# Expert 0's rows numbered by themselves; the routing of all experts computed at once inside expert 0's second block

## The chip, the core and the metric

The kernel runs on one core of one Trainium2 chip. The metric is the device time of one execution in microseconds (us), taken as the median over several timed executions. Besides the timed ones there is one profiled execution, whose trace is the source of every row quoted below. A core has five engines that run in parallel, each through its own instruction queue in order: TensorE (PE; PEld is its weight load), VectorE (DVE), ScalarE (ACT), GpSimd (POOL) and SyncE (SP, which here only starts DMAs). They wait for each other through semaphores.

## The reference, cut to what matters

Three stages follow one another: a packed attention, a mixture of experts with two of eight experts for each row, and a dense gated block.

```python
def _moe_ref(x, w_gate, w_noise, noise, w1, w2):      # x: 2304 rows of 512, the attention's output
    noisy_logits = x @ w_gate + np.log1p(np.exp(x @ w_noise)) * noise     # 2304 x 8
    top2 = np.argpartition(-noisy_logits, 2, axis=1)[:, :2]
    top2_l = np.take_along_axis(noisy_logits, top2, axis=1)
    top2_w = np.exp(top2_l - top2_l.max(-1, keepdims=True)); top2_w /= top2_w.sum(-1, keepdims=True) + 1e-09
    for e in range(8):
        for k in range(2):
            mask = top2[:, k] == e
            h = np.maximum(x[mask] @ w1[e], 0.0)
            out[mask] += top2_w[mask, k, None] * (h @ w2[e])
def _moe2_ref(x, w_in, w_out):
    h = x @ w_in
    return (h * (1 / (1 + np.exp(-h)))) @ w_out
```

## The kernel before

The 2304 rows are 18 row tiles of 128. Attention makes the row tiles two at a time (`unpacked`): scores `s`, a softmax on DVE, ACT and POOL (tiles `mx`, `sd`), transposes `a2p`, and the product `xp`, which gives a row tile (`xr`, written to the DRAM tensor `xs`) and its 16 gate and noise columns (`lg`). Attention's products are plain float32, the experts' are split into a high and a low part (three matmuls in float32r).

Routing (`route`) turns `lg` into a numbering. For each row: noisy logits `ny`, the two largest (`V.max`, `V.max_index`), one-hot rows `oh` and `ob`; a matmul with a triangle of ones (`rk`) counts the earlier rows of the same expert, so each row has a place in its expert's list. The list is turned inside out by matmuls `ip` of two one-hot factors (`oa`, 128 wide, and `oc`, 40 wide): place p of expert e then holds the row's index (`idx`). Routing runs in two chunks, row tiles 0 to 10 (`EARLY = 11`) and 11 to 17. From the same numbers come `slots` and `gates`, used only when the experts' results are combined, some 400 us later.

An expert's list has 640 places, handled as block A (2 tiles, 256 rows) and block B (3 tiles, 384 rows). A block gathers its rows from `xs` by an indirect DMA that POOL issues (`fetch`, one DMA for each tile of 128), transposes them on TensorE (`tps`), splits them into high and low (`xh` on ACT, `xl` on DVE; `xha` is block A's, `xhb` block B's), and then runs 8 steps f: `first` (12 matmuls into `hps`), `relu_split` (`hh` on ACT, `hl` on DVE), `second` (3 matmuls for each tile into `acc`; `wa4` to `wa7` are their weights, two steps to each). Block A of expert 0 needs only rows of the first chunk; block B needs the numbering of all rows.

Before the change, chunk one's numbering covers all experts, in steps spread over the last attention slots; chunk two's is spread over the steps of expert 0's block A; the rows of block B and of expert 1's block A are fetched after step 4 of block A. The scheduler of the framework then orders each engine's instructions. Expert 0's blocks use the weights `wa`, expert 1's `wb`; during expert 0's block B the weights of expert 1 are loaded and split (`split`, 1024 wide, ACT and DVE).

## Time and profile before

| | us |
|---|---|
| timed executions, median of 3 (lowest, highest) | 1002.8 (1000.08, 1003.62) |
| profiled execution, its own time | 994.48 |
| its span, first to last instruction | 992.6 |
| TensorE busy in the span | 962.6 |

The span is 1.9 us shorter than the profiled execution's own time, and that execution is 8.3 us shorter than the timed median, so terms are worked out on the trace and added to the median. A row of the timeline gives start, duration, engine, line, operation, what it writes and reads, its count, and in brackets how long its engine was idle before it and what ended the wait.

### The profile page before, as it was taken

The numbers are of one execution on the slowest core, as the hardware profiler recorded it, in microseconds if no ns is written. First come the engines' busy times: TensorE is split into PE (matmuls) and PEld (weight loads), VectorE is DVE, ScalarE is ACT, GpSimd is POOL, SyncE is SP. The second block draws the span as 40 slices with busy tenths as digits, with TensorE's granted clock in tenths as the row PEclk, the third lists the DMA queues.
The fourth block names the chain that finished last, engine by engine and source line by source line (L and its number), as shares of the span: only waits on it lengthen the run. The fifth ranks groups of instructions, "written<-read, shape, count | busy, mean of one in ns | idle before, by whom it ended". The sixth has DMA issues, their size and how long they took to land.

```text
span 992.6 us, 14383 instructions
## 1 busy us (share of the span) xinstructions
PE 962.6 (97%) x5584; PEld 825.5 (83%) x5584; DVE 447.7 (45%) x871; ACT 346.4 (35%) x631; POOL 312.8 (32%) x345
## 2 busy tenths in 40 slices
PE   6989799999999999999999999999999999999996
PEld 4767589999999999999999988888888888888885
DVE  3536763666767676676734448312212221111111
ACT  3657323443434433343423344322222222222221
POOL 2155214252424353352200127333323322222221
PEclk9979699999999999999999999999999999999999
DMA  8995223575657666665623455101011010001001
GB/s 234 249 265 165 92 86 106 183 239 179 217 187 231 191 216 215 199 222 184 193 94 118 141 174 163 54 22 43 22 51 35 23 53 1 1 1 43 0 1 46
DMA packets 82298, 122.49 MB, mean 123 GB/s; under 512 B 16432, under 2 KB 49200, under 8 KB 82224
## 3 DMA queue, kind: packets, MB, share of 16 engines
q1 hardware_dynamic: 74416, 101.05, 32.2%
q0 software_dynamic: 7520, 19.93, 6.9%
q8 instruction: 46, 0.75, 0.3%
q10 hardware_dynamic: 288, 0.52, 0.2%
q14 instruction: 28, 0.23, 0.1%
HBM read 93.17 MB, written 28.31 MB: 122 GB/s over the span
## 4 chain that ended last, share of the span: by engine, by line
PE 90%; DVE 4%; DMA 3%; ACT 1%; SPq 1%; issue 1%; DVEq 0%; ACTq 0%
PE hps L208 14%; PE hps L210 14%; PE hps L209 14%; PE acc L220 14%; PE acc L219 14%; PE acc L221 14%; PE xp L461 1%; PE s L430 1%; PE tps L157 1%; DMA vm<-in_v_dram 1%; PE s L363 1%; DMA km<-in_k_dram 1%; PE kp L352 1%; DVE rt_oa L535 1%; DMA raw<-wf_out 0%
## 5 line engine op out<-in xcount | busy, mean ns | idle before, releaser
L176 POOL DMA_INDIRECT xg<-xs,idx x120 | 126.6, 1055 | 195.5 <-DVE xturn L185 148.0
L751 POOL TENSOR_TENSOR gl<-sg,gh 128x512 fp32r<-128x512 f32 (+1 forms) x80 | 95.3, 1193 | 253.8 <-ACT gh L750 238.2
L232 ACT ACTIVATE hh<-hps 128x384 fp32r<-128x384 f32 (+1 forms) x128 | 56.1, 438 | 260.0 <-PE hps L210 256.3
L747 DVE TENSOR_TENSOR sg<-hps,sg 128x512 f32<-128x512 f32 (+1 forms) x80 | 50.7, 634 | 196.3 <-ACT sg L746 196.1
L233 DVE SCALAR_TENSOR_TENSOR hl<-hps,hh 128x384 fp32r<-128x384 f32 (+1 forms) x128 | 62.5, 488 | 122.9 <-ACT hh L232 122.3
L746 ACT ACTIVATE sg<-hps 128x512 f32<-128x512 f32 (+1 forms) x80 | 44.2, 553 | 190.2 <-PE hps L210 189.9
L750 ACT ACTIVATE gh<-sg 128x512 fp32r<-128x512 f32 (+1 forms) x80 | 47.1, 589 | 78.4 <-DVE sg L747 78.3
L737 POOL DMA_INDIRECT y<-ys,slots x36 | 36.5, 1014 | 110.7 <-DVE hl L233 72.5
L740 DVE TENSOR_SCALAR y<-y,gates 128x512 f32<-128x512 f32 x18 | 10.8, 602 | 38.2 <-DMA y<-ys,slots 38.2
L461 PE MATMUL xp<-ppBD,a2T 128*128 128x272 f32 (+1 forms) x80 | 25.5, 462 | 1.6 <-ACT xr L51 0.8
L741 DVE SCALAR_TENSOR_TENSOR y<-y,gates,y 128x512 f32<-128x512 f32 x18 | 15.7, 871 | 24.0 <-DMA y<-ys,slots 24.0
L690 DVE SCALAR_TENSOR_TENSOR t<-raw,t 128x512 int32<-128x512 int32 x32 | 22.2, 693 | 0.9
L196 POOL DMA_INDIRECT xg<-xs,idx x10 | 9.7, 969 | 40.9 <-DVE idx_f L556 19.4
L691 DVE SCALAR_TENSOR_TENSOR t<-raw,t 128x512 int32<-128x512 int32 x32 | 22.1, 691 | 0.9
L185 DVE STREAM_TRANSPOSE xturn<-xg 128x512 f32<-128x512 f32 x30 | 21.2, 707 | 2.6 <-DMA wf_in<-t 1.5
L687 ACT ACTIVATE t<-raw 128x512 f32<-128x512 f32 x32 | 21.2, 662 | 0.1
L430 PE MATMUL s<-ppT,qT 128*128 128x64 f32 x128 | 19.6, 309 | 0.0
L430 PEld LDWEIGHTS s<-ppT,qT 128*128 128x128 f32 x128 | 19.0, 227 | 0.6
L208 PE MATMUL hps<-xha,wa3h 128*128 128x256 f32 (+1 forms) x56 | 17.7, 316 | 1.8 <-DVE sg L747 1.8
L160 DVE TENSOR_TENSOR xla<-tps,xha 128x512 fp32r<-128x512 f32 x14 | 9.6, 690 | 21.1 <-ACT xha L159 21.0
L53 DVE COPY ysb<-acc 128x512 f32<-128x512 f32 x24 | 16.4, 683 | 4.8 <-PE acc L221 4.8
L352 PE MATMUL kp<-ident,km 128*128 128x128 f32 x64 | 12.0, 327 | 6.2 <-DMA km<-in_k_dram 5.8
(450 smaller groups left out, 2987.2 us busy)
## 6 DMA issues: line engine op xcount, KB each, us to landing
raw<-in_moe_w_dram SPq DMA_DIRECT2D x56, 512.0 KB, 3.9
ys<-ysb SPq DMA_DIRECT2D x40, 256.0 KB, 3.6
raw<-in_moe_w_in_dram SPq DMA_DIRECT2D x16, 512.0 KB, 4.2
raw<-in_moe_w_out_dram SPq DMA_DIRECT2D x16, 512.0 KB, 4.2
xs<-xr SPq DMA_DIRECT2D x18, 256.0 KB, 2.1
km<-in_k_dram SPq DMA_DIRECT2D x8, 512.0 KB, 7.5
vm<-in_v_dram SPq DMA_DIRECT2D x8, 512.0 KB, 7.5
qm<-in_q_dram SPq DMA_DIRECT2D x8, 512.0 KB, 7.1
```

Of the source, the lines that this page charges most:

```text
L176: G.indirect_dma_start(out=xg[:, g * P:(g + 1) * P], out_offset=None, in_=xs[:, :].rearrange("n (a f) -> (n a) f", a=4), in_offset=bass.In ...
L208: T.matmul(ps, wh[:, c, s], xh[:, c, :n], start=c == 0, stop=False)
L209: T.matmul(ps, wh[:, c, s], xl[:, c, :n], start=False, stop=False)
L210: T.matmul(ps, wl[:, c, s], xh[:, c, :n], start=False, stop=c == 3)
L219: T.matmul(y, hh[:, s], wh[:, f % 2, :], start=f == 0, stop=False)
L220: T.matmul(y, hh[:, s], wl[:, f % 2, :], start=False, stop=False)
L221: T.matmul(y, hl[:, s], wh[:, f % 2, :], start=False, stop=f == last)
L232: A.activation(hh, ps, AF.Relu)
L233: V.scalar_tensor_tensor(hl, ps, 0.0, hh.bitcast(F32), op0=OP.max, op1=OP.subtract)
L430: T.matmul(s2[:, :, h, :], qT[:, h, :], ppT[b, h // 4][:, h % 4], start=True, stop=True)
L747: V.tensor_tensor(sg, ps, sg, op=OP.mult)
L751: G.tensor_tensor(gl, sg, gh.bitcast(F32), op=OP.subtract)
```

## The change

- Chunk steps now number expert 0 alone (`first_rows`): a row counts if its expert 0 logit reaches its second largest, so `max_index`, `oh` and the 8-wide counts fall away; `rk` is n wide, `oc` 5 wide, `oa` one per row tile. Noisy logits stay in `ny`.
- Chunk one runs in one go in attention slot 9, and block A's rows are fetched at slot 12; chunk two's steps run after the last slot and give rows for block B alone (`idx0[:, TA:ET]`, 3 tiles), fetched before block A's loop in program order.
- A new `route()` inside expert 0's block B does what the old routing did for all 18 row tiles at once, with one `oa` and one `oc` instruction for each row tile and choice (36 of each, in tile `pc`). Expert 1's block A rows are fetched at step 4 of block B, those of its block B at step 6.
- `slots` and `gates` move there too; some constants are kept in working tiles.

```diff
-            for i in range(n):
-                V.max_index(i8[:, i, :], m8[:, i, :], ny[:, i, :])
-            ch = chosen[:, t0:t0 + n, :]
...
-            T.matmul(rk, ones, sbase[:, None, :].to_broadcast([P, n, E]), start=True, stop=False)
-            T.matmul(rk, ones, seen_b[:, None, :].to_broadcast([P, n, E]), start=False, stop=False)
-            T.matmul(rk, before, ob, start=False, stop=n == 1)
...
+            m0 = tl([], "m0", BF)
+            V.tensor_tensor(m0, yn[:, :, 0], m8[:, :, 1], op=OP.is_ge)
+            yield
+            rk = pMx.tile([P, n], F32, name="rk", tag="m")
+            T.matmul(rk, before, m0, start=True, stop=False)
...
+            V.scalar_tensor_tensor(sf, rk, -63.5, m0, op0=OP.add, op1=OP.mult)
...
+            for j in range(n):
+                V.tensor_scalar(oa[:, j, :], iota_lo, lo[:, j:j + 1], None, op0=OP.is_equal)
+            ip = pMx.tile([P, ET], F32, name="ip", tag="m")
+            for j in range(n):
+                T.matmul(ip, oa[:, j, :], oc[:, j, :], start=j == 0, stop=j == n - 1)
+            yield
+            if t0 == 0:
+                V.tensor_scalar(idx0[:, 0:TA], ip[:, 0:TA], float(-MID), float(MID), op0=OP.max, op1=OP.add)
...
+            else:
+                V.tensor_tensor(row0, row0, ip, op=OP.add)
+                V.tensor_scalar(idx0[:, TA:ET], row0[:, TA:ET], 0.0, float(N - 1), op0=OP.max, op1=OP.min)
...
-            if slot >= START2[5] + LAG2[3]:
-                run(r0, RSTEP)
+            if slot == START2[5] + LAG2[3]:
+                for _ in r0:
+                    pass
+            if slot == START2[-1]:
...
+                for j, xg in enumerate(fetch(xs[0:EARLY * P, :], idx0, 0, TA)):
+                    transposed(plain(xg), *X["a"], j)
+        for _ in r1:
             pass
...
+        for j, xg in enumerate(fetch(xs[:, :], idx0, TA, TB)):
+            transposed(plain(xg), *X["b"], j)
         for f in expert_block(0, 0, TA, X["a"]):
-            run(r1, 2)
...
+            pass
...
+                for i in range(NT):
+                    V.max(m8[:, i, :], ny[:, i, :])
+                for i in range(NT):
+                    V.max_index(i8[:, i, :], m8[:, i, :], ny[:, i, :])
...
+                            V.tensor_scalar(pc[:, j, c, 0:P], iota_lo, lo[:, t, c:c + 1], None, op0=OP.is_equal)
+                            V.tensor_scalar(pc[:, j, c, P:P + E * ET], iota_hi, hi[:, t, c:c + 1], rowv[:, t:t + 1],
+                                            op0=OP.is_equal, op1=OP.mult)
...
+                if e == 0:
+                    for _ in range(1 if f else 3):
+                        next(routing, None)
+                    if f == 4:
+                        box["a"] = fetch(xs[:, :], idx, ET, TA)
+                    if f == 6:
+                        for j, xg in enumerate(box["a"]):
+                            transposed(plain(xg), *X["a"], j)
...
-                if f == 5:
+                if f == (5 if e else 6):
```

**TensorE's queue from chunk one's counts to expert 0's block A.** Before (`rk` counts, `ip` inverts, `tps` and `hps` are block A's):

```order
L513 MATMUL rk<-rt_ob_1372,before 128x88
...
L461 MATMUL xp<-ppBD_185,a2T_1462 128x272
...
L430 MATMUL s_1634<-ppT_195,qT 128x2x32 x4
...
L452 MATMUL a2p<-ident,sd_1586 128x128 x4
...
L542 MATMUL ip<-rt_oc_1452,rt_oa_1451 128x40
...
L461 MATMUL xp<-ppBD_193,a2T_1675 128x272
...
L157 MATMUL tps<-ident,xg 128x128 x8
...
L208 MATMUL hps<-xha,wa0h 128x256
```

Now the same stretch:

```order
L502 MATMUL rk<-rt_m_1357,before 128x11
...
L506 MATMUL rk<-rt_m_1357,ones 128x1
L522 LDWEIGHTS rt_oa_1382
L522 MATMUL ip<-rt_oc_1379,rt_oa_1382 128x5
...
L388 MATMUL pp<-vm,a1T 32x64 x16
...
L460 MATMUL xp<-ppBD_184,a2T_1471 128x272
...
L156 MATMUL tps<-ident,xg 128x128 x8
...
L207 MATMUL hps<-xha,wa0h 128x256
```

Between `rk` and `ip` stood attention's `xp`, `s` and `a2p`; now nothing does, and the attention work follows `ip`. Eight `xp` products and six `a2p` transposes of the last row tiles now stand behind block A's first `hps`.

**GpSimd's queue around the fetch of block A's rows** (`ppBD<-px` are copies of attention's first half, `sd` a step of its softmax, `xg` the fetched rows). Before:

```order
L119 TENSOR_TENSOR wa7l<-raw,wa7h 128x256 x4
L397 COPY ppBD_197<-px 32x64 x4
L447 TENSOR_TENSOR sd_1586<-sd_1586,mx_1584 128x512
L196 DMA xg<-xs,idx_102 128x512 x2
L447 TENSOR_TENSOR sd_1645<-sd_1645,mx_1643 128x512
```

Now:

```order
L118 TENSOR_TENSOR wa7l<-raw,wa7h 128x256 x4
L396 COPY ppBD_196<-px 32x64 x4
L195 DMA xg<-xs,idx_99 128x512 x2
L446 TENSOR_TENSOR sd_1561<-sd_1561,mx_1559 128x512
L446 TENSOR_TENSOR sd_1625<-sd_1625,mx_1623 128x512
```

The two fetches moved ahead of one softmax step and stand right behind the four copies. The `px` that these copy needs the `pp` which now stands behind `ip` on TensorE.

**TensorE's queue from block A's last step to block B.** Before (`xhb` is block B's operand, `wa7` belongs to the last step):

```order
L221 MATMUL acc<-wa7h,hl 128x512 x2
L157 MATMUL tps<-ident,xg 128x128 x4
L219 MATMUL acc<-wa7h,hh 128x512
...
L221 MATMUL acc<-wa7h,hl 128x512 x2
L208 MATMUL hps<-xhb,wa0h 128x384
```

Now:

```order
L522 MATMUL ip<-rt_oc_1779,rt_oa_1782 128x5
L218 MATMUL acc<-wa7h,hh 128x512
...
L220 MATMUL acc<-wa7h,hl 128x512 x2
L752 LDWEIGHTS ones
L752 MATMUL rk<-sbase,ones 128x144
L156 MATMUL tps<-ident,xg 128x128 x12
L207 MATMUL hps<-xhb,wa0h 128x384
```

The transposes of block B's three tiles stood among block A's steps, with the last `tps` there being expert 1's; now they stand behind all of block A, six `acc` matmuls after the `ip` whose result gives their row indices.

## Rows read from the trace of the kernel before

**Rows 1.** The page: busy time by engine, and the chain that ended last.

```profile
PE 962.6 (97%) x5584; PEld 825.5 (83%) x5584; DVE 447.7 (45%) x871; ACT 346.4 (35%) x631; POOL 312.8 (32%) x345
PE 90%; DVE 4%; DMA 3%; ACT 1%; SPq 1%; issue 1%; DVEq 0%; ACTq 0%
```

**Rows 2.** Windows: length, busy PE, PEld, DVE, ACT, POOL (count), granted clock, DMA share, GB/s.

```profile
93.90:97.00 3.10, 3.10 (x71) 2.72 (x67) 2.99 (x7) 1.53 (x6) 3.06 (x6) 1.00 0.18 63
93.90:124.00 30.10, 23.76 (x198) 17.62 (x194) 24.31 (x102) 10.79 (x29) 12.38 (x21) 0.72 0.29 95
124.00:153.50 29.50, 28.79 (x230) 23.74 (x228) 17.98 (x85) 7.89 (x21) 4.76 (x5) 1.00 0.23 72
153.50:190.00 36.50, 36.50 (x194) 33.34 (x195) 13.76 (x19) 11.65 (x19) 11.43 (x11) 1.00 0.47 136
101.50:118.60 17.10, 13.05 (x80) 9.70 (x79) 14.66 (x45) 4.08 (x9) 4.31 (x6) 0.50 0.25 79
```

**Rows 3.** Windows of 1 us around changes of the granted clock.

```profile
53.00:54.00 1.00, 0.00 (x0) 0.00 (x0) 0.00 (x0) 0.80 (x1) 0.00 (x0) 0.88 1.00 255
64.00:65.00 1.00, 1.00 (x28) 0.83 (x30) 0.00 (x0) 0.91 (x3) 1.00 (x3) 1.00 1.09 359
101.00:102.00 1.00, 0.65 (x12) 0.51 (x10) 1.00 (x6) 0.34 (x1) 0.71 (x3) 0.77 0.00 0
118.00:119.00 1.00, 0.63 (x3) 0.21 (x3) 0.97 (x3) 0.00 (x0) 0.74 (x1) 0.70 0.64 139
```

**Rows 4.** Timeline of VectorE, chunk one's numbering.

```profile
92.95 0.20 DVE L483 TENSOR_SCALAR rt_h<-rt_w 128x88 f32<-128x88 f32 x1
...
97.53 0.84 DVE L498 MAX8 rt_m<-rt_ny 128x8 f32<-128x8 f32 x11
...
99.85 0.76 DVE L578 TENSOR_TENSOR rt_ex<-rt_m 128x11 f32<-128x11 f32 x1
...
109.97 3.29 DVE L535 TENSOR_TENSOR rt_oa<-iota_lo,rt_lo 128x768 f16<-128x768 f16 x4
```

**Rows 5.** Timeline of TensorE, end of attention to block B.

```profile
91.14 1.08 PE L461 MATMUL xp<-ppBD,a2T 128*128 128x272 f32 x4
...
101.52 0.56 PE L515 MATMUL rk<-rt_ob,ones 128*128 128x80 bf16 x10
...
120.70 1.04 PE L157 MATMUL tps<-ident,xg 128*128 128x128 f32 x8
...
137.95 0.55 PE L542 MATMUL ip<-rt_oc,rt_oa 128*128 128x40 f16 x8 [0.55 <-DVE rt_oa L535]
...
140.70 0.49 PE L560 MATMUL i<-idx_f,ident 128*32 128x40 f32 x32
...
153.46 0.44 PE L208 MATMUL hps<-xhb,wa0h 128*128 128x384 f32 x1
...
157.73 0.39 PE L219 MATMUL acc<-wa4h,hh 128*128 128x512 f32 x1
157.96 0.40 PE L220 MATMUL acc<-wa4l,hh 128*128 128x512 f32 x1
```

**Rows 6.** Timeline of GpSimd, copies and fetches.

```profile
100.52 1.27 POOL L397 COPY ppBD<-px 32x64 f32<-32x64 f32 x4
...
139.24 0.98 POOL L196 DMA_INDIRECT xg<-xs,idx  x1 [19.43 <-DVE idx_f L556]
140.52 0.95 POOL L196 DMA_INDIRECT xg<-xs,idx  x1 [0.31 <-issue]
```

**Rows 7.** The fetch's line, L196: DMA to landing.

```profile
DMA to landing us min/median/max: 3.4/3.5/4.0
```

**Rows 8.** Timeline of ScalarE and VectorE: the split of fetched rows.

```profile
121.74 1.08 ACT L159 ACTIVATE xha<-tps 128x512 fp32r<-128x512 f32 x2
...
123.06 0.68 DVE L160 TENSOR_TENSOR xla<-tps,xha 128x512 fp32r<-128x512 f32 x1
```

**Rows 9.** Groups of VectorE instructions from 98.2 to 99.84 us: busy, mean ns.

```profile
L500 DVE FIND_INDEX8 rt_i<-rt_m,rt_ny 128x8 uint32<-128x8 f32 x11 | 1.5, 160 | 0.0
```

More of the change, by code (lines that the diff above doesn't have):

```diff
@@ L89, in body @@
     slots = const.tile([P, NT, 2], I32)
-    seen = const.tile([P, E], F32)
-    V.memset(seen, 0.0)
-    seen_b = const.tile([P, E], BF)
-    V.memset(seen_b, 0.0)
+    ny = const.tile([P, NT, E], F32)
     idx_f = const.tile([P, E * ET], F32)
@@ L96, in body @@
     idx = const.tile([P, E * ET], I32)
-    idx0 = const.tile([P, TA], I32)
+    idx0 = const.tile([P, TA + TB], I32)
     idx4 = const.tile([P, 4, E * ET], I32)
@@ L101, in body @@
         V.memset(quad[32 * a:32 * a + 32], float(a))
-    few = const.tile([P, E], F32)
+    few = const.tile([P, 1], F32)
+    cnt = const.tile([P, E], F32)
+    most = const.tile([P, 1], I32)
     M = {"pin": False, "w": 384, "hb": 3}
@@ L513, in route @@
-            T.matmul(rk, before, ob, start=False, stop=n == 1)
+            rk = pMx.tile([P, n], F32, name="rk", tag="m")
+            T.matmul(rk, before, m0, start=True, stop=False)
+            if t0:
+                T.matmul(rk, ones, seen_b.to_broadcast([P, n]), start=False, stop=False)
             for j in range(n - 1):
-                T.matmul(rk[:, j + 1:, :], ones, ob[:, j:j + 1, :].to_broadcast([P, n - 1 - j, E]),
-                         start=False, stop=j == n - 2)
-            rs = tl([E], "rs")
@@ L518, in route @@
-            V.tensor_scalar(rs, rk, -63.5, None, op0=OP.add)
-            V.tensor_tensor(oh, oh, rs[:, :, None, :].to_broadcast([P, n, 2, E]), op=OP.mult)
-            sf, hi, hs, lo = tl([2], "sf"), tl([2], "hi"), tl([2], "hs"), tl([2], "lo")
-            V.tensor_reduce(sf, oh, axis=AX.X, op=OP.add)
+                T.matmul(rk[:, j + 1:], ones, m0[:, j:j + 1].to_broadcast([P, n - 1 - j]), start=False, stop=j == n - 2)
+            sf, hi, hs, lo = tl([], "sf"), tl([], "hi"), tl([], "hs"), tl([], "lo")
@@ L539, in route @@
-            ip = pMx.tile([P, E * ET], F32, name="ip", tag="m")
-            for j in range(n):
-                for c in range(2):
-                    T.matmul(ip, oa[:, j, c, :], oc[:, j, c, :], start=j + c == 0, stop=j == n - 1 and c == 1)
-            if t0 + n < NT:
-                V.tensor_tensor(idx_f, idx_f, ip, op=OP.add)
-                V.tensor_scalar(idx0, idx_f[:, 0:TA], 0.0, float((t0 + n) * P - 1), op0=OP.max, op1=OP.min)
-                sn = rt.tile([P, E], F32, name=f"sn{n}")
-                V.tensor_reduce(sn, ob.rearrange("p n e -> p e n"), axis=AX.X, op=OP.add)
-                V.tensor_tensor(seen, seen, sn, op=OP.add)
-                V.tensor_copy(seen_b, seen)
-                c = pMx.tile([P, E], F32, name="c", tag="m")
+            oc = tl([ET], "oc", F16)
@@ L612, in run @@
                 next(gen, None)
[L614 removed]
+        r0 = first_rows(0, EARLY, lgs[0])
+        r1 = first_rows(EARLY, NT - EARLY, lgs[EARLY])
         W[0] = []
@@ L653, in body @@
         tick()
-        r1 = route(EARLY, NT - EARLY, lgs[EARLY])
-        for i in "ab":
-            X[i] = tuple(xp_.tile([P, 4, BW], F32R, name=f"x{c}{i}", tag=f"x{c}{i}") for c in "hl")
-        for j, xg in enumerate(fetch(xs[0:EARLY * P, :], idx0, 0, TA)):
-            transposed(plain(xg), *X["a"], j)
-        cnt = const.tile([P, E], F32)
-        most = const.tile([P, 1], I32)
-        rows = []
-        for f in expert_block(0, 0, TA, X["a"]):
-            run(r1, 2)
-            if f == 4:
-                for _ in r1:
-                    pass
-                rows = fetch(xs[:, :], idx, TA, TB) + fetch(xs[:, :], idx, ET, TA)
-                c = pMx.tile([P, E], F32, name="c", tag="m")
-                T.matmul(c, ones, seen_b, start=True, stop=True)
-                V.tensor_tensor(cnt, c, few, op=OP.max)
-                V.tensor_reduce(most, cnt, axis=AX.X, op=OP.max)
-            if f > 4:
-                transposed(plain(rows[f - 5]), *X["b"], f - 5)
+        for j, xg in enumerate(fetch(xs[:, :], idx0, TA, TB)):
+            transposed(plain(xg), *X["b"], j)
+        for f in expert_block(0, 0, TA, X["a"]):
+            pass
         flush(0)
-        for j in range(TA):
-            transposed(plain(rows[TB + j]), *X["a"], j)
     def load64(raws, sbuf, src, last=None):
@@ L784, in routed @@
             wi, wo = W[0], W[1]
             first_rows = combine(0)
+            routing = route()
             box = {"b": []}
```

150 lines of the change are left out of this document (92 added, 58 removed).

## The prediction

> **What bounds the kernel now.** I read the page first: TensorE is busy for 962.6 us of the span of 992.6, and nine tenths of the chain that ended last are its own work [rows 1]. So a part of the change counts only by what it does to TensorE's waits, its clock or its amount of work. The windows then show where that is open: from the end of attention to expert 0's block A (93.9 to 124.0) TensorE is busy for 23.76 of 30.10 us, during block A for 28.79 of 29.50, and from block B on for all of it [rows 2]. What is lost ahead of block B is therefore never regained, and what is saved there is kept whole. [...] What makes TensorE wait there is VectorE's numbering of chunk one, whose pieces the timeline gives [rows 4].
>
> **The change, part by part.** I follow three marks on TensorE: block A's first `hps` (124.0 before), its last `acc`, and block B's first `hps` (153.46) [rows 5], then what block B has to carry.
>
> *1. Block A starts earlier.* The noisy logits and the eleven `MAX8` stay; these end at 98.4 [rows 4]. Now a single comparison of 11 elements follows. Its price lies between one of the `MAX8` (0.84 / 11 = 0.08 us) and the 0.76 us that a subtraction of the same shape took at 99.85 while GpSimd was splitting weights, as it will be now [rows 4]; I take 0.5, so 98.9. Eleven `rk` matmuls, as ten took 0.56 [rows 5]: 99.5. Six small VectorE steps in a row (`sf`, `hi`, `hs`, `oc`, `lo`, `oc`) at 0.20, a small `TENSOR_SCALAR` with nothing overlapped [rows 4]: 100.7. Eleven `oa` of 128 columns: four of 768 took 3.29 us, 0.137 for each 128 [rows 4], so 1.5 (bounds 0.08 and 0.20 each, from the rows above: 0.9 to 2.2). With the last `ip` block A's indices are there at about 102.4.
>
> TensorE's queue has only `rk` and `ip` in this stretch, so it idles from some 97 to 102, more than before, and I expect the clock to fall as it did at 101.5 after a far fuller stretch [rows 3]. Behind `ip` stands attention work: the window's 23.76 us are 17.2 at full clock; minus 2.0 for the old `rk` and `ip` (11 at 0.056 and 22 at about 0.065), 2.2 that is done by 97 (3.1 [rows 2] without the 0.9 of `pp`, which moves), and 4.4 that moved behind block A's start (eight `xp` at 0.46 and six transposes at 0.11 [rows 5]) leaves 8.6 us. At full clock throughout, TensorE would be through by 111.0, but the rows are not there: GpSimd issues the fetches only behind the four `ppBD` copies, so `pp` 0.9, `px` 0.35, copies 1.27 [rows 6], two fetches 1.28 us apart [rows 6], landing 3.5 us after issue [rows 7], then transposes and split, 120.70 to 123.74 [rows 5, 8], with some overlap 2 to 3 us: 112. At half clock throughout: 102.4 + 17.2 = 119.6. The two earlier falls lasted 10.2 us (53.9 to 64.0) and 17.1 us [rows 3]; with ten, half clock ends near 111.7 and block A starts near 115. I take 115: **-9** (bounds -12 and -4).
>
> *2. Block A is a little longer.* Into it go eight `xp` and six transposes, 4.4 us; out of it go 20 transposes of fetched rows (2.0 us by the 8 in 1.04, overlap taken off), the 32 small `i` instructions (0.42), most of `ip` and the 0.55 us wait for it [rows 5]. With short waits for `hh` where nothing fills them: **+0.8**.
>
> *3. Block B waits for its rows.* `ip` of chunk two stands six `acc` matmuls before block A's end. Those take 1.4 us (0.23 each [rows 5]), and nothing else is queued ahead of block B's transposes. Meanwhile: from the end of the old `ip` (138.5) to the first fetch at 139.24 it took 0.7 [rows 5, 6]; the third fetch follows 2.55 later [rows 6], lands after 3.5 [rows 7], and its transposes, ScalarE's half of the split and VectorE's 0.68 take about 1.9 [rows 5, 8]. That makes 8.6 us from `ip` to a flowing block B; minus 1.5: **+7.1**. Before, these fetches were issued at 139.24, 14 us ahead of block B. Queued behind the waiting transposes is all of TensorE's work, so nothing hides it.
>
> [...]
>
> *4. The clock behind that wait.* TensorE stands still for 2.6 us and then works in pieces of half a microsecond. After 2 to 3 us of standing still the clock fell before (no work at all from 53 to 54 [rows 3]), and came back 4.6 us (from 114 to 118.6) or 9.2 us (54.8 to 64.0) after the work was dense again. Half of either is lost: 2.3 to 4.6. I take **+3.3**; the lower bound is 0, if the clock holds.
>
> *5. The chosen experts.* Block B's third matmul group is now `rk`, which needs `ob`. On VectorE that stands behind the last row split, eight `MAX8`, eighteen index searches at 0.135 (eleven in 1.5 us [rows 9]) and four small steps: some 4.7 us after block B's first `hps`. The two steps ahead of `rk` take 4.3 us at full clock (153.46 to 157.73 [rows 5]) and more at half: **+0.5** (0 to 3).
>
> *6. Work moved into block B*, where TensorE has no idle time to put it in: 19 `rk` at 0.056 (1.1), 36 `ip` at 0.05 to 0.07 (2.1), the `i` matmuls (0.45), and the 8 transposes of expert 1's block A (0.83), all at the durations of [rows 5]: **+4.5**. What it replaced is counted out in steps 1 and 2.
>
> *7. VectorE in block B.* It was busy for 13.76 of 36.5 us there [rows 2], so 22.7 are free. The routing needs 36 `oa` at 0.137 and 36 `oc` of 40 columns at about 0.12 (9.3 us), the searches and maxima (3), and some 25 small or middle steps (6 to 7): 19 us. It is hidden as long as it stays in order with the splits of expert 1's weights; the price if that cover is gone is what exceeds 22.7, at 0.20 for every `oa` and `oc` some 2 us, and the wait of the `hl` steps behind it. At the end the last step of block B no longer overlaps expert 1's first; its second row tile is transposed and split just ahead of the first `hps`: **+1.0** (0 to 5).
>
> [...]
>
> Sum: -9 + 0.8 + 7.1 + 3.3 + 0.5 + 4.5 + 1.0 = **+8.2**. On the trace that is a span of 1000.8 (own time 1002.7); on the timed median, 1002.8 + 8.2 = **1011**.
>
> **Rivals.** *The clock holds (no change).* [...] Then step 1 is -12 and step 4 is 0: +1.9, 1004.7. For it: the clock survived the gaps from 97 to 101. Against: each fall in this trace followed a gap smaller than or like the new ones [rows 3].
>
> *VectorE is late in block B.* Steps 5 and 7 at their upper bounds, +6.5 more: 1017.5. For it: the queue puts `hl` behind up to 24 `pc` instructions. Against: 22.7 us free.
>
> *Half clock explains the longer timed executions (faster).* The timed ones take 8.3 us more than the profiled one. If in those the half clock of the tail does not end at 118.6 but goes on into block A, each us of it costs half a us, and the changed kernel, which reaches block A's dense matmuls 9 us sooner, could be spared it. To undo +8.2 and win 0.5% (5 us) the stretch would have to last 26 us longer, to about 145; then 1011 - 13.2 = 997.8 or less. The 8.3 us account for 17 us of it, and by that the result is 1002.7. [...] Against: no row shows where the 8.3 us are.
>
> *The numbering was not what TensorE waited for.* Then block A starts no earlier than POOL and attention allow, step 1 is -4 and the sum +13: 1016. The gaps at `rk` and `ip` speak against it.
>
> **How the numbers follow.** Forecast with its neighbours, VectorE late and a weak step 1 included: 0.62 slower (forecast alone 0.42, VectorE late 0.12, weak start 0.08). Clock holds: 0.26, no change. Longer half clock before: 0.12, faster. About 0.5%, 5 us, is what a measurement of this kernel can tell from no change (its three times lie 3.5 us apart). The range goes from 1000, which takes in the clock rival and leaves out most of the faster one, to 1018, which takes in the late VectorE.
>
> **What would show it.** In the changed kernel's trace: chunk one's `ip` ending near 102 and block A's first `hps` near 115 (step 1; 110 or 120 would be wrong); a wait of TensorE of 5 to 6 us, in pieces, at the `tps` ahead of block B, ended by the fetch (step 3); the granted clock at half behind it (step 4); a short wait for `ob` (step 5); no long wait for `pc` (step 7); expert 1's block B starting some 8 us later than before. The prediction fails if block B starts before 146, if that wait is under 3 us, or if TensorE's clock never falls after 95 us.

## The result, and the profile after

The changed kernel takes 1014.15 us (median of 4, 1012.23 to 1018.66) beside 1002.41 us before on the same chip (1000.08 to 1003.62): ratio 1.0126, 95% interval 1.0086 to 1.0167. It is slower, as forecast, and by 11.7 us instead of the +8.2. Its profiled execution took 1012.84 us, span 1011.0: 18.4 more than the span before. So I also ran it a second time on another chip ("again", below): ratio 1.0138, 13.5 us between the timed medians, span 1006.3, 13.7 more than before. The chips differ (the kernel before took 994 to 995 us on three of them, 1002 and 1004 on two), and ratios from different chips are not compared more finely than that here; for that the traces are used.

The page of the changed kernel and, in the second fence, of the second execution (answers to [rows 1]):

```profile
PE 972.2 (96%) x5618; PEld 831.1 (82%) x5618; DVE 454.3 (45%) x961; ACT 346.5 (34%) x630; POOL 313.6 (31%) x345
PE 86%; DMA 5%; issue 3%; SPq 2%; DVE 2%; ACT 1%; POOL 1%; DVEq 0%; POOLq 0%; ACTq 0%
```

```profile
PE 966.8 (96%) x5618; PEld 826.6 (82%) x5618; DVE 456.8 (45%) x961; ACT 346.7 (34%) x630; POOL 315.8 (31%) x345
PE 89%; DMA 4%; DVE 2%; issue 1%; SPq 1%; ACT 1%; POOL 0%; DVEq 0%; ACTq 0%; POOLq 0%
```

TensorE is busy for 4 to 10 us longer and idle for 9 us longer than in [rows 1], and transfers take a larger part of the chain. Windows of the second execution, cut at the same places of the program as [rows 2]: attention's end, block A, the gap ahead of block B, block B, start of expert 1.

```profile
93.90:117.10 23.20, 18.61 (x197) 14.47 (x195) 15.40 (x63) 7.15 (x20) 10.58 (x19) 0.71 0.35 103
117.10:146.50 29.40, 29.40 (x191) 24.65 (x189) 11.54 (x62) 9.11 (x24) 2.29 (x3) 0.99 0.13 46
146.50:156.00 9.50, 2.98 (x15) 1.99 (x14) 3.35 (x17) 2.39 (x4) 2.26 (x3) 0.77 0.43 139
156.00:189.80 33.80, 33.80 (x192) 28.16 (x193) 29.39 (x153) 7.45 (x12) 0.00 (x0) 0.91 0.18 48
189.80:203.00 13.20, 11.23 (x92) 9.21 (x91) 6.67 (x10) 4.56 (x7) 9.77 (x9) 1.00 0.83 258
```

Ahead of block B there is now a gap of 9.5 us in which TensorE works for 2.98; before there was none. VectorE, busy for 13.76 us in block B before, is now busy for 29.39 of 33.80. The pieces of the gap in TensorE's timeline, second execution (answers to [rows 5]; the first row is chunk one's `ip`, the second block A's transposes):

```profile
101.03 1.65 PE L522 MATMUL ip<-rt_oc,rt_oa 128*128 128x5 f16 x10
113.53 1.82 PE L156 MATMUL tps<-ident,xg 128*128 128x128 f32 x8 [1.13 <-DMA xg<-xs,idx]
...
144.78 0.33 PE L522 MATMUL ip<-rt_oc,rt_oa 128*128 128x5 f16 x7
...
149.38 0.66 PE L156 MATMUL tps<-ident,xg 128*128 128x128 f32 x4 [1.86 <-DMA xg<-xs,idx]
152.17 1.97 PE L156 MATMUL tps<-ident,xg 128*128 128x128 f32 x8 [2.13 <-DMA xg<-xs,idx]
155.97 0.69 PE L207 MATMUL hps<-xhb,wa0h 128*128 128x384 f32 x1 [1.83 <-DVE xlb L159]
```

The three waits, 5.8 us together, are the ones that the prediction asked for, at the place that it named. The first two are ended by the fetched rows, the third by VectorE's half of their split.

Four marks show where the time went: TensorE's first `hps` of block A, of block B, of block B's second weight tile, and of expert 1's block A at its third weight tile (`wb2`). From there on the second execution keeps its distance to the end. Start times in us; `idx` is when VectorE's write of expert 1's indices begins (before, these came from the old numbering). The prediction put block A's start before at 124.0; that is the second product of its loop, and the first stands 1.1 us earlier:

```profile
122.88 0.38 PE L208 MATMUL hps<-xha,wa0h 128*128 128x256 f32 x1 [0.22 <-ACT xha L159]
```

In rows_known and rows_and_pair some of block B's first products stand among block A's, so its start is left out.

| kernel | block A | block B | B, tile 2 | idx | expert 1, tile 3 | span |
|---|---|---|---|---|---|---|
| before | 122.88 | 153.46 | 159.12 | | 196.66 | 992.6 |
| changed | 113.97 | 152.65 | 160.21 | 186.12 | 212.65 | 1011.0 |
| changed, again | 117.10 | 155.97 | 163.69 | 189.62 | 210.60 | 1006.3 |
| rows_known | 114.33 | | 156.34 | 191.38 | 210.55 | 1006.7 |
| rows1_known | 116.92 | 155.90 | 163.64 | 189.55 | 209.91 | 1006.8 |
| one_pair | 116.30 | 156.13 | 162.94 | 170.79 | 203.56 | 1001.1 |
| rows_and_pair | 115.56 | | 157.40 | 172.38 | 198.47 | 994.6 |
| filled_wait | 113.28 | 152.00 | 157.68 | 168.10 | 197.69 | 995.3 |
| attention_first | 112.42 | 143.97 | 155.39 | 189.65 | 215.23 | 1015.2 |
| grouped | 114.61 | 153.48 | 160.60 | 191.39 | 217.37 | 1014.7 |
| two_parts | 117.72 | 153.94 | 160.78 | 173.23 | 201.62 | 998.3 |
| two_parts_attention_first | 115.99 | 149.69 | 159.88 | 178.57 | 200.40 | 996.7 |
| two_parts_own_ysb | 115.48 | 149.09 | 156.67 | 176.42 | 198.55 | 996.0 |
| two_parts_idx_first | 113.94 | 149.02 | 156.60 | 176.36 | 198.05 | 995.5 |

### The profile page after: what moved, and what is told of

It reads as the page before. It is cut to its first block, busy times and chain, and to the rows that moved or that the text cites. A ratio compares the mean times of both kernels' runs of the same rounds, so it can differ in the third digit from the quotient of the medians.

```text
span 1011.0 us, 14536 instructions
## 1 busy us (share of the span) xinstructions
PE 972.2 (96%) x5618; PEld 831.1 (82%) x5618; DVE 454.3 (45%) x961; ACT 346.5 (34%) x630; POOL 313.6 (31%) x345
## 4 chain that ended last, share of the span: by engine, by line
PE 86%; DMA 5%; issue 3%; SPq 2%; DVE 2%; ACT 1%; POOL 1%; DVEq 0%; POOLq 0%; ACTq 0%
PE hps L207 14%; PE hps L208 14%; PE hps L209 14%; PE acc L218 13%; PE acc L219 13%; PE acc L220 13%; DMA xg<-xs,idx 1%; PE xp L460 1%; PE tps L156 1%; DMA raw<-in_moe_w_dram 1%; DMA vm<-in_v_dram 1%; SPq L277 1%; PE s L362 1%; DMA km<-in_k_dram 1%; PE s L429 1%
## 5 line engine op out<-in xcount | busy, mean ns | idle before, releaser
L460 PE MATMUL xp<-ppBD,a2T 128*128 128x272 f32 (+1 forms) x80 | 23.3, 434 | 0.2 <-ACT a2T L51 0.2
L207 PE MATMUL hps<-xhb,wa0h 128*128 128x384 f32 (+1 forms) x48 | 18.3, 381 | 1.6 <-DVE xlb L159 1.6
L429 PEld LDWEIGHTS s<-ppT,qT 128*128 128x128 f32 x128 | 17.2, 209 | 1.5 <-PE xp L460 1.1
```

Of the source, the lines that this page charges most:

```text
L207: T.matmul(ps, wh[:, c, s], xh[:, c, :n], start=c == 0, stop=False)
```

## The experiments

My theory was the prediction's: two separate losses that add up, block B's late rows with the slow clock behind them, and the work put into block B. The rival: something else, running beside the first loss, is late at expert 1 in any case.

**again: the changed kernel once more, on another chip.**

> The changed kernel once more, unaltered. Its first profiled execution was 18.4 us longer than that of before, the timed median only 11.7. In that profile ScalarE, VectorE and GpSimd stood still together between 204.4 and 211.8 us, with no releaser that the trace can name, and TensorE behind them. Theory A (that stall belonged to this one execution): the new profile lacks it, TensorE goes from expert 1's second to its third weight tile without an idle stretch, the span is 1005 to 1007 us, and the timed ratio stays near 1.012. Rival B (it is part of the kernel): it is there again at the same instruction, the span is 1010 to 1012 us.

Ratio 1.0138 (1.0117 to 1.0159), 1007.99 us, and the long stall is gone: theory A. Up to the first steps of expert 1 the two executions agree within 0.5 us once their starts are allowed for (they lie 3.1 to 3.5 us apart, of which 2.95 are there at chunk one's `MAX8` already); there the first one has waits of 3 to 7 us that this one has not. They are taken up under what stays open.

**rows_known: block B's rows from chunk one's indices alone,** so that their fetch waits neither for chunk two's numbering nor for its rows.

```diff
+                V.tensor_scalar(row0, ip, float(MID), None, op0=OP.add); V.tensor_scalar(idx0[:, TA:ET], row0[:, TA:ET], 0.0, float(EARLY * P - 1), op0=OP.max, op1=OP.min)
...
-                V.tensor_scalar(idx0[:, TA:ET], row0[:, TA:ET], 0.0, float(N - 1), op0=OP.max, op1=OP.min)
...
-        for j, xg in enumerate(fetch(xs[:, :], idx0, TA, TB)):
+        for j, xg in enumerate(fetch(xs[0:EARLY * P, :], idx0, TA, TB)):
```

> Block B's rows are fetched by numbers that chunk one alone gives, so they are there long before block B (they are not the reference's rows; all other work is left as it was). Forecast by steps 3 and 4 of the prediction: the wait of TensorE ahead of block B (8.6 us between block A's last acc and block B's flowing in the trace) and the half clock behind it (2.7 us) go: 10 to 12 us less than the changed kernel, ratio to before 0.999 to 1.004, no half clock after 115 us. Rival (something else is late then, chunk two's noisy logits and with them the numbering of all experts): only 3 to 6 us less, ratio 1.006 to 1.010, with a wait for ob or pc in block B.

Ratio 1.0171 (1.0154 to 1.0189): no gain at all. My theory was wrong here, and the rival stronger than I had written it. The wait ahead of block B did go (its second weight tile starts 7.4 us earlier than in the second execution, 2.8 of them from an earlier block A), and waits of 1.09 and 6.46 us stand at block B's end (another, of 3.0, is ahead of block B's first `acc`; see two_parts_own_ysb). TensorE's timeline there, and VectorE's last step of the routing, in two fences:

```profile
189.74 0.49 PE L790 MATMUL i<-idx_f,ident 128*32 128x40 f32 x32 [1.09 <-DVE idx_f L784]
196.69 1.97 PE L156 MATMUL tps<-ident,xg 128*128 128x128 f32 x8 [6.46 <-DMA xg<-xs,idx]
```

```profile
191.38 0.17 DVE L785 CAST idx<-idx_f 128x40 int32<-128x40 f32 x1
```

TensorE reaches expert 1 earlier and finds no rows, because VectorE has the indices no sooner than before.

**rows1_known: expert 1's rows from expert 0's indices,** known long before; the routing runs as it did, only the rows no longer wait for it, and the order of TensorE's queue stays.

```diff
-                        box["a"] = fetch(xs[:, :], idx, ET, TA)
+                        box["a"] = fetch(xs[:, :], idx0, 0, TA)
...
-                    box["b"] = fetch4(c0, TB) if e else fetch(xs[:, :], idx, c0, TB)
+                    box["b"] = fetch4(c0, TB) if e else fetch(xs[:, :], idx0, TA, TB)
```

> Expert 1's rows, of both blocks, are fetched by expert 0's numbers, which are known before block B begins (so they are not the reference's; the routing in block B is computed as before this edit). The order on TensorE, VectorE and ScalarE is unchanged. Forecast by step 7 (end of block B): what TensorE waits for at the end of block B is the chain from the last ip over the fetch, the transposes and the split; without it 3 to 5 us less than the changed kernel, ratio 1.007 to 1.010. Rival (the row tiles are there in time, and the wait is for ScalarE's and VectorE's queues in their given order): less than 1 us, ratio 1.011 to 1.014.

Ratio 1.0136 (1.0115 to 1.0156), 0.7 us less at expert 1's third tile: the rival is right. TensorE's waits at the end of block B in the second execution show how little there was to gain:

```profile
194.77 0.66 PE L156 MATMUL tps<-ident,xg 128*128 128x128 f32 x4 [0.54 <-DMA xg<-xs,idx]
...
200.08 0.50 PE L207 MATMUL hps<-xha,wb0h 128*128 128x256 f32 x2 [0.56 <-ACT xha L158]
201.45 0.39 PE L208 MATMUL hps<-xla,wb0h 128*128 128x256 f32 x1 [0.87 <-DVE xla L159]
```

Only the first, 0.54 us, is a wait for fetched rows, and it is gone in rows1_known. The other two are for the split of the second row tile, whose transposes stand behind block B's last `acc` in TensorE's queue; they are there in rows1_known too (0.56 and 0.87). Undoing either wait alone gives nothing or next to nothing: TensorE reaches expert 1's rows within 0.54 us of their landing, so the two chains end at nearly the same time.

**one_pair: block B inverts one of the 36 pairs.** 35 `oa`, 35 `oc` and 35 `ip` are left out; the rows gathered for expert 1 are others, no transfer falls away.

```diff
-                for j0 in range(0, NT, 3):
+                for j0 in (NT - 3,):
...
-                    for j in range(3):
+                    for j in (2,):
...
-                        for c in range(2):
+                        for c in (1,):
```

> Of the 36 pairs of oa, oc and ip in block B only one is left (the numbers are then not the reference's; rk, the slots and the gates stay). Forecast by step 6 of the prediction, 0.06 us for each ip: 2.1 us less from these, and about 2 to 3 more because expert 1's rows can be fetched earlier: ratio 1.007 to 1.009. Rival (an ip costs TensorE more between the matmuls of block B, 0.13 us as the spacing of 0.30 in place of 0.17 us there suggests): 4.4 us from these and 3 to 4 from the earlier rows, ratio 1.004 to 1.006.

Ratio 1.0058 (1.0039 to 1.0076). From block B's second tile to expert 1's third it takes 40.62 us instead of 46.91 (by the table): 6.3 less, and the rival, by which an `ip` costs more where it stands than in a row, is right. (With the rows there earlier TensorE's 2.0 us of waits at block B's end are gone too, and its transposes stand further ahead in the queue.) Its price can be read in the second execution's timeline of TensorE and of its weight loads:

```profile
173.18 0.19 PE L779 MATMUL ip<-pc 128*128 128x40 f16 x1
173.22 0.42 PE L207 MATMUL hps<-xhb,wa2h 128*128 128x384 f32 x1
173.48 0.19 PE L779 MATMUL ip<-pc 128*128 128x40 f16 x1
173.52 0.42 PE L208 MATMUL hps<-xlb,wa2h 128*128 128x384 f32 x1
...
183.10 0.34 PE L208 MATMUL hps<-xlb,wa3h 128*128 128x384 f32 x1
183.28 0.34 PE L209 MATMUL hps<-xhb,wa3l 128*128 128x384 f32 x1
```

```profile
178.30 0.10 PEld L779 LDWEIGHTS <-pc 128*128 128x128 f16 x1
178.31 0.20 PEld L208 LDWEIGHTS hps<-xlb,wa2h 128*128 128x128 f32 x1
178.43 0.19 PEld L209 LDWEIGHTS hps<-xhb,wa2l 128*128 128x128 f32 x1
```

With an `ip` between them two `hps` start 0.30 us apart (173.22, 173.52), with none 0.17 to 0.18 (183.10, 183.28). The loads show why: the weights of the `hps` behind an `ip` are loaded only when that `ip` starts (178.30, 178.31; this `hps` itself starts at 178.34), those of the next one well ahead of its start (178.43 for 178.60). So a lone `ip` costs 0.13 us. Over the whole of block B, the 36 (six of them in a row) lengthen the spacing of the `hps` and `acc` around them by 3.9 us in all (each spacing less its usual 0.17 or 0.23, summed).

**rows_and_pair: both cuts together.** The same edits as in rows_known and one_pair.

> Both edits together: block B's rows by chunk one's numbers (there long before block B) and one of the 36 pairs. Alone, the first gained 7.3 us up to block B's last weight tile and lost all of it at the end of block B in a wait of 6.5 us for expert 1's rows; the second gained 7.0. Theory (VectorE's chain of routing, some 35 us from the first MAX8 to the finished numbers, sets the end of block B as soon as block B starts earlier): with the chain cut short the two gains add, 13 to 17 us less than the changed kernel, ratio to before 0.997 to 1.001, and no wait for rows at the end of block B. Rival (the first edit lost its gain because block B's matmuls were drawn into block A): the gain of the second alone stays, ratio 1.005 to 1.008.

Ratio 0.9940 (0.9923 to 0.9957), below even the theory's range, on a chip where the kernel before took 1003.66. By the traces it is 2.0 us longer than the kernel before (span 994.6), so the timed gain rests on the longer timed runs of that one, which stay open (below). Beside one_pair the span is 6.5 us shorter. With the routing's chain short, the same early rows that gave nothing in rows_known give 5.1 us at expert 1's third tile. The two losses lie side by side, and the later one counts.

**filled_wait: the gap ahead of block B filled with bf16 matmuls** that nobody reads (29, in three pieces ahead of, between and behind the transposes, whose order is fixed with them), pair cut as in one_pair, rows fetched as in the changed kernel.

```diff
+        def fill(n):
+            ps = pMx.tile([P, 4, P], F32, name="fill", tag="m")
+            for i in range(n):
+                tc.keep_in_program_order(T.matmul(ps, ones, ones[:, None, :].to_broadcast([P, 4, P]), start=i == 0, stop=i == n - 1))
...
+        fill(12)
+        transposed(plain(late[0]), *X["b"], 0)
+        fill(9)
+        transposed(plain(late[1]), *X["b"], 1)
+        transposed(plain(late[2]), *X["b"], 2)
+        fill(8)
```

> On the kernel with one pair, 29 matmuls whose result nobody reads (128x512, bf16) stand on TensorE in the three gaps between block A's last acc and block B's first hps, so TensorE is not idle while the rows come. Step 4 of the prediction: the half clock at the start of block B (0.84 on average from 153 to 175 us in the kernel with one pair) comes from standing still, so with the gaps filled it goes; block B starts within 1 us of where it did, then 2 to 3.5 us less than one pair alone, ratio 1.002 to 1.004. Rival (the clock falls there for another reason, or the filling only delays the transposes): no half clock removed, ratio 1.005 to 1.008.

Ratio 0.9981 (0.9968 to 0.9995), below both ranges, but on the same chip as rows_and_pair, where the kernel before is longer; its control one_pair ran on another. So the traces decide: span 995.3, 5.8 less than one_pair's, of which 3.0 are there at block A's start already, ahead of the edit. The granted clock in filled_wait, from 1 us behind its first block B `hps` on; in one_pair over the same window; and around the gap in the second execution of the changed kernel:

```profile
153.00:165.00 12.00, 12.00 (x80) 11.15 (x80) 8.60 (x59) 3.01 (x6) 0.00 (x0) 1.00 0.01 1
```

```profile
153.00:165.00 12.00, 10.34 (x61) 9.42 (x60) 9.24 (x74) 2.39 (x5) 0.00 (x0) 0.71 0.00 1
```

```profile
152.00:153.00 1.00, 0.83 (x4) 0.71 (x4) 0.00 (x0) 0.00 (x0) 0.00 (x0) 0.50 0.20 78
155.00:156.00 1.00, 0.03 (x1) 0.03 (x1) 1.00 (x9) 0.00 (x0) 0.00 (x0) 0.50 0.03 8
...
160.00:161.00 1.00, 1.00 (x5) 1.00 (x4) 0.81 (x5) 0.49 (x1) 0.00 (x0) 0.50 0.00 0
162.00:163.00 1.00, 1.00 (x8) 0.83 (x7) 0.00 (x0) 0.00 (x0) 0.00 (x0) 1.00 0.00 0
```

Unfilled, TensorE's granted clock is 0.50 in the last eight transposes and the first steps of block B (second execution, 152 to 161); filled, it is 1.00. What the clock costs is read from the same work in each: block B's first 24 `hps`, up to the first other product. The stretch from the first to the second tile in the table does not hold the same work: in some kernels six `acc` stand in it, in others the `rk`. TensorE in filled_wait, in one_pair and (its first `hps` at 155.97 is shown above) in the second execution:

```profile
152.00 0.44 PE L207 MATMUL hps<-xhb,wa0h 128*128 128x384 f32 x1 [0.26 <-DVE xlb L159]
...
156.29 0.39 PE L218 MATMUL acc<-wa4h,hh 128*128 128x512 f32 x1
```

```profile
156.13 0.69 PE L207 MATMUL hps<-xhb,wa0h 128*128 128x384 f32 x1 [1.46 <-DVE xlb L159]
...
162.22 0.24 PE L753 MATMUL rk<-ob,before 128*128 128x144 bf16 x1
```

```profile
162.97 0.24 PE L753 MATMUL rk<-ob,before 128*128 128x144 bf16 x1
```

They take 4.29 us filled, as before (4.27, 153.46 to 157.73 in [rows 5]), 6.09 in one_pair and 7.00 in the second execution. So in block B the clock costs 1.8 us in one_pair and 2.7 in the changed kernel, and filling the gap undoes it.

**attention_first: the last attention work ahead of block A's steps** and not spread over them, so that chunk two's numbering comes earlier.

```diff
+        block = expert_block(0, 0, TA, X["a"])
+        for _ in range(2):
+            next(block)
+        with tc.issue_after(M["xp"].ins):
+            next(block)
+        for _ in r1:
+            pass
```

> The changed kernel with one order changed: attention's last xp matmuls are issued ahead of the third step of block A, instead of one group behind each of its steps. So chunk two's noisy logits are complete some 8 us earlier, its ip stands two steps ahead of block A's end, and the rows are fetched before block A ends; TensorE idles up to 2 us among the xp. All work is done, all rows are the reference's. Theory (attention's spread xp, not the numbering itself, made block B's rows late, and the routing chain starts earlier too): no wait of TensorE ahead of block B, no half clock behind it, 7 to 11 us less than the changed kernel, ratio 1.003 to 1.007. Rival (VectorE's chain of routing sets block B's end whatever its start): the wait moves to the end of block B as it did with rows known, ratio 1.010 to 1.015.

Ratio 1.0161 (1.0138 to 1.0184). Outside both ranges, but with the rival's mechanism: chunk two's `ip` runs at 133.22 instead of 144.78 and block B starts at 143.97 with no wait for its rows, 9.5 us ahead of the kernel before, and all of it is lost again. VectorE's indices come at 189.65, as in the second execution. TensorE's timeline in block B, at its first `acc` and at its end:

```profile
152.67 0.79 PE L218 MATMUL acc<-wa4h,hh 128*128 128x512 f32 x1 [2.75 <-ACT hh L231]
...
195.16 1.97 PE L156 MATMUL tps<-ident,xg 128*128 128x128 f32 x8 [6.44 <-DMA xg<-xs,idx]
```

**grouped: the `ip` of twelve pairs in a row,** three such runs, each a step behind its `pc`, instead of one by one.

> The 36 ip of block B stand in three runs of 12 in a row, each one step behind the pc that it reads, instead of one by one between hps and acc. Theory (an ip alone costs 0.13 us because the next hps can't load its weights ahead of it; in a row it costs the 0.063 us of the kernel before): 2 to 3 us less than the changed kernel, ratio 1.010 to 1.012. Rival (the end of block B waits for the routing chain, which this edit lengthens by holding the last ip back): same or up to 3 us more, ratio 1.013 to 1.017.

Ratio 1.0177 (1.0157 to 1.0197). Twelve `ip` in a row lengthen the spacing of the `acc` around them by 0.32 us, 0.03 each, so TensorE saves 2.9 us of the 3.9. All of it is lost in a wait of 6.31 us for expert 1's rows, since `idx` comes at 191.39, 1.8 later than in the second execution. The rival is right, and by a little more than it said.

**two_parts: all experts' numbering of row tiles 0 to 10 in block A's steps, only tiles 11 to 17 in block B.** This and the three that follow do all the work of the reference.

```diff
+        def early_rows():
+            n = EARLY
...
+            for j in range(n - 1, -1, -1):
+                for c in range(2):
+                    T.matmul(ip, oa[:, j, c, :], oc[:, j, c, :], start=j == n - 1 and c == 0, stop=j == 0 and c == 1)
+            V.tensor_tensor(idx_f, idx_f, ip, op=OP.add)
...
-            def route():
+            def route(t0=EARLY, n=NT - EARLY):
```

> All work done, rows as in the reference. The numbering of all experts is split: chunk one's eleven row tiles (11 MAX8, 11 searches, 22 ip, their slots and gates) go into block A, where VectorE is busy for only 10 of 28 us, and only chunk two's seven tiles (14 of the 36 pairs) stay in block B; expert 1's rows are fetched one step earlier. Theory (VectorE's chain of routing in block B, 35 us, and TensorE's own work up to there are nearly equally long, so both must be shortened): the chain falls to some 20 us and no longer sets block B's end; the 22 ip stand in a row where TensorE waits for rows anyway, so 3 to 7 us less than the changed kernel, ratio 1.006 to 1.010. Rival (the work is only moved, block A gets longer by what block B loses): ratio 1.012 to 1.015.

Ratio 1.0063 (1.0039 to 1.0088), on a chip where the kernel before took 993.93. As the theory said. The indices come at 173.23, and the waits for expert 1's rows are gone; block B is still not ahead of the kernel before.

**two_parts_attention_first** adds attention_first's edit to it, and issues the first three steps of the early numbering in one go.

> The split numbering and attention's last xp ahead of block A's third step, together. Alone the second gained 9 to 12 us up to block B's first matmul and lost it all at the end of block B, where the routing chain was not ready. Theory: with the chain cut the gain stays, as with rows and pair (0.994, which left 35 pairs out): 10 to 14 us less than the changed kernel, ratio 0.999 to 1.004. Rival (the chain still sets the end, or block B's first hh waits for block A's ysb to be written, as it did for 2.8 us): ratio 1.006 to 1.012.

Ratio 1.0087 (1.0064 to 1.011), in the rival's range; the interval overlaps that of two_parts: no gain that can be told.

**two_parts_own_ysb** keeps that edit and gives block A's result tiles a buffer apart, since the routing's first `MAX8` in block B waits for their write to memory in some of the runs (rows_known's row):

```profile
153.66 0.64 DVE L739 MAX8 rt<-ny 128x8 f32<-128x8 f32 x8 [2.88 <-DMA ys<-ysb]
```

```diff
-                    ysb = M["s"].tile([P, DM], F32, name="ysb", tag="ysb", bufs=3)
+                    ysb = M["s"].tile([P, DM], F32, name="ysb", tag="ysb", bufs=3) if M["lag"] else \
+                        raws.tile([P, 1024], F32, name="ysb", tag="raw")[:, 0:DM]
```

> As two parts with attention first, and block A's two ysb tiles lie in the pool of the raw weights, so that block B's tiles need not wait until these are written to memory. Theory (that wait, 2.8 us at block B's first hh and 2.9 at the first MAX8 with attention first, is left as the last one ahead of block B): another 2 to 4 us less, ratio 0.996 to 1.001, below before. Rival (the weight loads behind the two raw tiles come later and TensorE waits for them): the same as the former or slower by up to 2 us.

Ratio 1.0048 (1.0032 to 1.0064), outside the theory's range: block B's second tile is 3.2 us earlier than without the buffer, expert 1's third tile 1.9, since a wait of 1.38 us for expert 1's rows comes back.

**two_parts_idx_first** keeps both and issues the early numbering on VectorE only behind chunk one's indices.

```diff
-        run(er, 3)
+        with tc.issue_after(M["i0"].ins):
+            run(er, 3)
```

> The two-part version with ysb in a buffer of its own, and in addition VectorE's early numbering of all experts is issued only behind the indices of expert 0's chunk one. It does all the work of the reference. Theory: chunk one's ip waits 2.9 us there for rt_oa instead of 1.2 because the early numbering stands ahead of it on VectorE; with that order undone block A of expert 0 starts 1.7 us earlier and everything behind it too: ratio to the kernel before 1.001 to 1.004, span about 994.5. Rival: block A's start is bound by the fetches, which GpSimd issues behind its ppBD copies, whatever VectorE does: ip ends earlier, block A does not, ratio 1.004 to 1.006 as without this edit.

Ratio 1.0032 (1.0020 to 1.0044). The wait of chunk one's `ip` is 1.21 instead of 2.89 us and block A starts 1.5 us earlier, but at expert 1's third tile only 0.5 is left: block B starts at 149.02 and 149.09, and TensorE's waits for chunk two's rows grew from 0.84 to 1.36 us. So the ratio falls where the theory said (its interval overlaps that of two_parts_own_ysb), and most of the gain is lost by block B. None of the versions that do all the work beats the kernel before; this is the nearest.

## Why the prediction was right, step by step

The sign held, and so did the waits and the clock that were forecast ahead of block B. Three sizes were wrong: block A's early start (step 1), the price of the `ip` (step 6) and the end of block B (step 7). The steps beside what the traces show (differences to the kernel before, by the table's marks; step 4 is block B's first 24 `hps`, like for like):

| steps | forecast | changed | again |
|---|---|---|---|
| 1, block A's start | -9 | -8.9 | -5.8 |
| 2 and 3, block A and the wait for rows | +7.9 | +8.1 | +8.3 |
| 4, clock behind the wait | +3.3 | +2.6 | +2.7 |
| 5 to 7, from there to expert 1's third tile | +6.0 | +14.2 | +8.7 |
| sum | +8.2 | +16.0 | +13.9 |

On the spans the forecast was 5.5 us too low in the second execution (+13.7) and 10.2 in the first (+18.4), on the first set's timed medians only 3.5 (+11.7). That it lies so near there is partly luck: in that set the kernel before is timed some 8 us above its profile, for a reason that stays open.

*Step 1* holds with a smaller size: -5.8 instead of -9 in the second execution. Part of the difference between the executions is older than the change: `MAX8` starts at 95.18 in the first, at 98.13 in the second, at 97.53 before [rows 4]. Counted from `MAX8`, block A starts 6.4 to 6.6 us earlier, within the bounds and below my value; 1.1 of the difference is the mark that I had read too late (124.0). (The 17.2 us at full clock in my value are the window's 23.76 less half of the 13.05 that lie where the granted clock is 0.50, both in [rows 2].) The indices are as early as I said (`MAX8` done at 98.97, `idx` at 102.71 in the second execution: 3.7 against 4.0). The missing part is GpSimd's: the fetches stand behind a weight split, which stood in the order shown with the change and which I had not counted. `px`, which the copies read, is written by 104.47 (first fence), and the copies start at 106.57 (second):

```profile
104.12 0.35 DVE L391 TENSOR_SCALAR px<-pp,mx 128x128 f32<-128x128 f32 x1 [1.18 <-PE pp L388]
```

```profile
103.86 2.78 POOL L118 TENSOR_TENSOR wa7l<-raw,wa7h 128x256 fp32r<-128x256 f32 x4 [5.39 <-issue]
106.57 1.04 POOL L396 COPY ppBD<-px 32x64 f32<-32x64 f32 x4
107.90 1.16 POOL L195 DMA_INDIRECT xg<-xs,idx  x1 [0.29 <-POOL ppBD L396]
```

That was the fourth rival's mechanism in part (block A no earlier than GpSimd allows), with 2.1 of the 5 us that it set against mine. Why GpSimd stands idle for 5.39 us ahead of the split the trace does not say.

*Steps 2 and 3* hold together. From its first `hps` block A takes 29.4 us instead of 30.6, so -1.2 where I had +0.8, and the gap to block B is 9.5 us instead of my 7.1. What I left out of it is that the last eight of its transposes run at a granted clock of 0.50 (152 to 153), 1.97 us against 1.04 for eight in [rows 5].

The 3.5 us that I took from a fetch's issue to its landing held: in the second execution the first fetch of chunk two is issued at 145.88 and its transposes start at 149.38, 3.5 later.

*Step 4*: mechanism shown by filled_wait (granted clock 1.00 from 153 to 165 with the gap filled, 0.71 in one_pair), +2.6 and +2.7 instead of +3.3, within its bounds. The rival in which the clock holds falls with it.

*Step 5* did not come up: `ob` was ready in time, TensorE does not wait at `rk`, and +0.5 becomes 0.

*Step 6* is mis-sized: +4.5 counted the 36 `ip` at 0.05 to 0.07 us as they stood in a row in [rows 5]. Placed one by one between the `hps` they cost up to 0.13 each, 3.9 us together and not 2.1.

*Step 7* failed in its argument, and in the changed kernel that cost little. I compared the sum of VectorE's work, 19 us, with its 22.7 free us in block B and called it hidden. The sum was right: 29.39 us busy there, less the `hl` steps and the splits that VectorE does for expert 1, which are some 10 (the 36 pairs of `oa` and `oc` took more than I had, 0.37 us from one to the next (173.11 to 173.48) or some 13 in all instead of 9.3, the rest less). But what counts is when the last step of the routing is done, since expert 1's rows need another 7 us behind it (`idx` to `tps`' end in rows_known: 191.38 to 198.66). In order among `hl` and splits, the routing takes from 154.56 to 189.62, and these are its first and last rows:

```profile
154.56 0.77 DVE L739 MAX8 rt<-ny 128x8 f32<-128x8 f32 x10
...
189.62 0.18 DVE L785 CAST idx<-idx_f 128x40 int32<-128x40 f32 x1
```

The largest part of it, the groups of VectorE's instructions between 154 and 190 us:

```profile
L775 DVE TENSOR_SCALAR pc<-iota_hi,rt,rowv 128x40 f16<-128x40 f32 x36 | 10.4, 297 | 0.0
L774 DVE TENSOR_SCALAR pc<-iota_lo,rt 128x128 f16<-128x128 f16 x36 | 8.4, 247 | 0.1
```

So the second rival (VectorE late in block B) was right in kind, with another victim: not the `hl` steps wait, but expert 1's rows. In the second execution TensorE idles for 2.0 us at the end of block B (busy for 11.23 of 13.20 in the last window above). Of these 0.54 are the wait for the rows; 1.43 are the one that step 7 had named, the second row tile split just ahead of the first `hps`, and priced at 1.0. The late routing shows its weight where TensorE reaches the end of block B earlier: 6.3 to 6.5 us of waits for the rows in rows_known, attention_first and grouped. The 8.7 us of the last part are then 3.9 for `ip`, 2.3 for the rest of step 6 (`rk` 0.7, `i` 0.5, transposes 1.1; 2.4 forecast) and 2.0 idle, which leaves 0.5 without a name.

And the steps do not add as I added them. Up to block B's end there are two chains: TensorE's own (late rows, clock, `ip`) and VectorE's routing, which ends at about the same time. rows_known and attention_first shorten the first alone and gain nothing, rows1_known takes the rows off the second alone and gains 0.7; one_pair shortens both, and rows_and_pair still more.

**What stays open.** The first execution has waits at expert 1's first steps that the second has not: ScalarE and GpSimd stand still with no cause that the trace names. ScalarE, then GpSimd, of the first execution:

```profile
211.75 0.38 ACT L231 ACTIVATE hh<-hps 128x256 fp32r<-128x256 f32 x1 [7.38 <-remote]
```

```profile
212.73 0.94 POOL L175 DMA_INDIRECT xg<-xs,idx  x1 [2.04 <-remote]
```

attention_first and grouped have the like (7.43 and 4.59 us of ScalarE), filled_wait and rows_and_pair shorter ones (1.61 of ScalarE, 3.30 of VectorE), and the others none. I found no cause. From block B's start to expert 1's third tile the first execution takes 5.4 us longer than the second, 3.2 of them idleness of TensorE, and it loses another 2.7 behind; that is what sets its 18.4 against 13.7. Open as well is why the kernel before takes 8 to 9 us longer in its timed executions than in its profile in two of the sets of runs and not in the three others. The third rival offered half clock for it, of which the change would spare a part. The record has the mean granted clock of most of these runs: 0.980 in the set where the kernel before took 1003.66, 0.982 to 0.984 in those of 994 to 995. By my estimate that is 1 to 4 us of lost time ((1 - clock) times the span), so half clock explains less than half of the 9. Whether the change spares a part of it the ratios, 1.0126 in a set with the longer times and 1.0138 in one without, lie too close to tell.

## What to carry to other kernels

Work that is moved under a busy engine is not hidden because the engine beside it has that much free time: ask when its last step is done, and what has to follow before somebody needs it, here 7 us of fetch, transpose and split. When two chains end together, an experiment that removes one shows nothing; remove both before you call either harmless. And price a small matmul by the place where it will stand: between products of another kind the `ip` cost 0.11 us on average (3.9 for 36), where I had priced it at 0.05 to 0.07 from a row of its like.

## What the runs showed of the hardware

A lone f16 `ip` between float32r matmuls cost 0.13 us (second execution: `hps` 0.30 us apart with one between them, 0.17 to 0.18 with none), and the weights behind it were loaded only when it started (178.31 and 178.30); twelve in a row cost 0.03 each (grouped: 0.32 us in all). The small VectorE instructions were slower than I had scaled them from large ones: eleven `oa` of 128 columns took 1.87 us in the second execution, 0.17 each where I took 0.137. And bf16 matmuls that nobody reads, put into a gap of 9 us, kept TensorE's granted clock at 1.00 from 153 to 165, where it was 0.71 without them, and were worth 1.8 us in the 24 products behind it (filled_wait against one_pair: 4.29 and 6.09).
